# ScalarE makes one of the last chunk's two copies and two of the last six stores

## The chip, the cores and the metric

The kernel runs on one core of a Trainium2 chip. The time is the device time of one execution in microseconds (us), as the median of several runs. The core has five engines that run side by side, each with its own ordered list of instructions: TensorE (PE: matmuls), VectorE (DVE), ScalarE (ACT), GpSimd (POOL) and SyncE (SP). A transfer (DMA) is issued by an engine from its list, here by SP or by ScalarE, and is then carried out by 16 DMA engines that all queues share.

## The reference

Two stages. The first is a linear attention with a sketched feature map; the second takes its output, with the four heads side by side, as 4352 tokens of 128 values and sends them through a two-layer network with the activation h * sigmoid(beta * h):

```
q, k, v: 4 x 4 x 1088 x 32 (batch, heads, sequence, head size);  S1, S2: 8 x 32
phi(x) = outer product of S1 x and S2 x, 64 features
num = phi(q) (phi(k)^T v);  den = phi(q) . sum over the sequence of phi(k);  x = num / (den + 1e-6)
x -> 4352 x 128;  h = x @ w_in (128 x 2048);  g = h / (1 + exp(-beta * h));  out = g @ w_out (2048 x 128)
```

The output is 4352 x 128 in float32.

## The kernel before

Only the end of the second stage matters here. The tokens are worked off in ten chunks (`tok_chk`), numbered 0 to 9: chunks 0, 2 and 9 have 256 tokens, the others 512. Chunk 9 is `LAST`; chunk 8 holds tokens 3584 to 4095, and chunk 9 tokens 4096 to 4351.

For a chunk the 2048 hidden values come as 16 blocks of 128. `W` (line 384) makes the first layer's matmuls for a group of blocks into a PSUM tile `wave` (L393). `S` (line 407) has ScalarE apply Silu to it, giving the fp16 tile `g` (L410). `V` (line 418) adds the second layer's product to the accumulator `moeout`: for chunks 0 to 8 with the weights as the stationary operand (L440), so that the result is feature by token. For chunk 9 the operands are exchanged (L428), the result is token by feature, and its two halves of 128 tokens stand in two PSUM tiles, `moe["acc"][0]` and `moe["acc"][1]`. Within each `V` of chunk 9 the matmuls of the first half come before those of the second.

`y` (`turn_out`, line 453) takes a finished accumulator to an SBUF tile `o_sb`, of which there are two, used in turn. For chunks 0 to 8 it is one 32 x 32 block transpose on VectorE (L463). For chunk 9 it is two plain copies on VectorE, one for each half (L460).

`z` (`store_out`, line 467) sends the oldest tile that has not been sent to the output. Up to chunk 8 it calls `store` (line 362), which issues four DMAs on SP, one for each group of 32 partitions (L369); a chunk that crosses the end of a batch entry is cut in two and takes eight. Chunk 8 does not cross one and takes four of 64 KB. For chunk 9, `z` issues two DMAs on SP, one for each half, 64 KB each (L474).

The order of the work is written out by hand: `SEQ` (line 890) is a list of tokens, each of which calls one of these functions. It fixes the order of each engine's own instructions. Between engines nothing but data holds them: each instruction waits for those whose tiles it reads or overwrites, and these waits are put in from the reads and writes. `y` and `z` work through first-in-first-out lists (`done`, `outs`), so that the k-th `z` stores the chunk that the k-th `y` turned. The list before ends in

```
V W V S W V S S V y z V V y z z
```

where the first `y` is chunk 8's, the first `z` chunk 7's, the second `y` chunk 9's, and the last two `z` are those of chunks 8 and 9. The last `S` stands ahead of all of these.

Of the kernel before, what the change touches and what calls it, by code (L numbers as in the profile page):

```python
# [15 lines left out]
P = 128  # L16
# [3 lines left out]
def kernel(  # L20
# [14 lines left out]
    B, H, S, D = q.shape  # L35
# [24 lines left out]
    tok_chk = []  # L60
# [43 lines left out]
    PE, DVE, ACT, POOL, SP = nc.tensor, nc.vector, nc.scalar, nc.gpsimd, nc.sync  # L104
    DO = {}

    def op(name):
        def put(fn):
            assert name not in DO, name
            DO[name] = fn  # L110
            return fn

        return put
# [244 lines left out]
    LAST = len(tok_chk) - 1  # L358
# [3 lines left out]
    def store(o_sb, t0, nt):  # L362
        c = t0
        while c < t0 + 32 * nt:
            b, r = divmod(c, S)
            n = min(t0 + 32 * nt - c, S - r) // 32
            u = (c - t0) // 32
            for g4 in range(4):
                SP.dma_start(  # L369
                    out=bass.AP(  # L370
                        tensor=out.tensor,
                        offset=out.offset + (b * S + r // 32) * DM + 32 * g4,
                        ap=[[T * DM, 32], [DM, n], [1, 32]],
                    ),
                    in_=o_sb[32 * g4 : 32 * g4 + 32, u : u + n, :],
                )
            c += n * 32
# [74 lines left out]
    @op("y")  # L452
    def turn_out():
        ci, t = done.pop(0)
        t0, tw = tok_chk[ci]
        o_sb = sbA.tile([P, TCH // 32, 32], F32, tag="o_sb", name="o_sb")
        nt = tw // 32
        if ci == LAST:
            for n in range(tw // P):
                DVE.tensor_copy(out=o_sb[:, 4 * n : 4 * n + 4, :].rearrange("p t d -> p (t d)"), in_=t[n][:, :P])  # L460
            outs.append((ci, o_sb, t0, nt))
            return
        DVE.transpose(out=o_sb[:, :nt, :].rearrange("p t d -> p (t d)"), in_=t[:, :tw])  # L463
        outs.append((ci, o_sb, t0, nt))

    @op("z")
    def store_out():
        ci, o_sb, t0, nt = outs.pop(0)
        if ci < LAST:
            store(o_sb, t0, nt)  # L470
            return
        b, r = divmod(t0, S)
        for n in range(nt // 4):
            SP.dma_start(  # L474
                out=bass.AP(
                    tensor=out.tensor,
                    offset=out.offset + (b * S + r // 32 + 4 * n) * DM,
                    ap=[[T * DM, 32], [DM, 4], [1, DM]],
                ),
                in_=o_sb[:, 4 * n : 4 * n + 4, :],  # L480
            )
# [60 lines left out]
    for b in range(B):  # L542
# [57 lines left out]
        if b == 0:  # L600
# [36 lines left out]
            for c, (j0, j1) in (("a", (0, 2)), ("b", (2, NJK))):  # L637
                r = slice(H * j0, H * j1)
                n = H * (j1 - j0)
# [227 lines left out]
    for n, (j0, j1) in enumerate(JRP):  # L867
# [34 lines left out]
        DI3 O33 S V V W y v30 v31 S W S v32 S DS3 W V z W S V W v33 v34 S W V kt3 S W p30 S V t30 W V  # L902
        nd3 S W p33 t33 S S V P31 W V S t31 P32 t32 V W y S n3 V W V V x30 X31 W S S V W V S W S V W S V
        W V W V V S S W W V S S V y W z V W V S S W S V W V W V S W S V W S V W z V S W S V W V S y W S
        V W V S W V S S V y z V V y z z
    """
    for s_ in SEQ.split():
        DO[s_]()
# [29 lines left out]
```

## Time and profile before

| | us |
|---|---|
| median of 3 runs | 109.79 |
| the runs | 109.72, 110.7, 109.79 |
| the profiled execution | 110.03 |
| its span, first to last instruction | 108.2 |
| around the span (110.03 - 108.2) | 1.83 |

In the span, TensorE has matmuls for 98.6 us (91%), ScalarE is busy for 72.8 us (67%), VectorE for 63.4 us (59%) and GpSimd for 33.8 us (31%). TensorE's granted clock is 1.0 throughout.

How to read the lines: times are us from the span's start unless they are marked ns; "L369" is line 369 of the kernel before. "SPq" and "ACTq" are instructions that SP's and ScalarE's sequencers handle themselves, issues of DMAs above all; "ACT" and "DVE" without q are the engines' own work. A timeline line has the start, the length, engine, line, operation, output <- input, and the count of instructions merged; in square brackets stands the idle time before it and what ended it. A line by source or tile has shortest/median/longest ns and the first and last start. "DMA to landing" is the time from the start of a DMA's issue to its completion. In a line of windows the first fields are the stretch and its length, then busy time (and count) of PE, PEld, DVE, ACT and POOL, and at the end the granted clock, the mean busy share of the 16 DMA engines, and GB/s.

### The profile page before, as it was taken

Reading aid. Unit: us, or ns where it says so; the run is one execution under the profiler, and the core shown is the slowest. Engines: PE = TensorE matmul, PEld = TensorE weight load, DVE = VectorE, ACT = ScalarE, POOL = GpSimd, SP = SyncE. Lnnn points to the kernel's source line nnn. Section 1 sums busy time; section 2 is a strip of 40 time slices with the busy share of each in tenths; the row PEclk is TensorE's granted clock in tenths of the full one; section 3 lists DMA queues with packets and bytes.
Section 4 is the critical chain, followed back from the end, with each engine's and each line's share of the span. In section 5 each row is a group of like instructions: output and inputs, shape, how many; then the busy total and the mean of one; then the engine's idle time right before and its main releaser. Section 6 shows DMA issues by size and latency. Waiting matters only on the chain.

```text
span 108.2 us, 2920 instructions
## 1 busy us (share of the span) xinstructions
PE 98.6 (91%) x1205; PEld 55.4 (51%) x1205; DVE 63.4 (59%) x115; ACT 72.8 (67%) x90; POOL 33.8 (31%) x51
## 2 busy tenths in 40 slices
PE   6999969977996999999999999999998999999940
PEld 2443327463653746648545545556554555556830
DVE  3056999999999999999920255807825020110210
ACT  0520001267989755798999746999965999999920
POOL 5002949991893305653910002090000000000000
PEclk9999999999999999999999999999999999999999
DMA  3999999989501451002741224060014005014061
GB/s 76 366 254 373 412 386 247 321 255 357 211 9 27 127 134 23 6 0 48 158 117 32 45 36 64 0 97 21 18 21 69 15 7 84 13 27 70 0 97 49
DMA packets 23517, 12.65 MB, mean 117 GB/s; under 512 B 19408, under 2 KB 21712, under 8 KB 23504
## 3 DMA queue, kind: packets, MB, share of 16 engines
q1 hardware_dynamic: 22896, 11.88, 40.7%
q10 hardware_dynamic: 608, 0.59, 2.2%
q8 instruction: 9, 0.15, 0.6%
q14 instruction: 4, 0.03, 0.1%
HBM read 9.94 MB, written 2.23 MB: 112 GB/s over the span
## 4 chain that ended last, share of the span: by engine, by line
PE 52%; DVE 40%; issue 3%; ACT 1%; DVEq 0%; ACTq 0%
PE wave L393 19%; PE moeout L440 19%; DVE qo L529 7%; PE kvz L267 5%; DVE kp L529 5%; DVE qT L487 4%; DVE kT L487 3%; DVE qt L741 3%; PE nps L756 3%; DVE kab L557 3%; DVE qab L701 3%; PE moeout L428 2%; PE kvs L793 1%; DVE o_sb L463 1%; DVE qm L707 1%
## 5 line engine op out<-in xcount | busy, mean ns | idle before, releaser
L410 ACT ACTIVATE g<-wave 128x1024 f16<-128x1024 f32 x68 | 65.4, 1034 | 10.0 <-PE wave L393 9.9
L393 PE MATMUL wave<-xT,winp 128*128 128x512 f16 (+1 forms) x160 | 40.3, 351 | 1.2 <-DVE winp L332 0.7
L440 PE MATMUL moeout<-g,woutp 128*128 128x512 f16 (+1 forms) x144 | 35.9, 355 | 0.9 <-DVE woutp L346 0.4
L393 PEld LDWEIGHTS <-winp 128*128 128x128 f16 x160 | 21.0, 146 | 14.7 <-issue 2.6
L440 PEld LDWEIGHTS <-woutp 128*128 128x128 f16 x144 | 13.7, 97 | 13.6 <-issue 2.3
L463 DVE STREAM_TRANSPOSE o_sb<-moeout 128x512 f32<-128x512 f32 (+1 forms) x9 | 5.8, 644 | 23.2 <-PE moeout L440 23.2
L529 POOL TENSOR_TENSOR kp<-kab 128x512 f32<-128x512 f32 (+1 forms) x13 | 13.2, 1042 | 12.5 <-DVE kab L557 9.6
L267 PE MATMUL kvz<-idle 128*128 128x384 f16 x41 | 11.0, 412 | 1.1 <-DVE hm L238 1.1
L529 POOL TENSOR_TENSOR qo<-qab 128x512 f32<-128x512 f32 (+1 forms) x7 | 8.8, 1265 | 3.6 <-DVE qab L725 3.5
L529 DVE TENSOR_TENSOR qo<-qab 128x512 f32<-128x512 f32 (+2 forms) x10 | 9.6, 970 | 0.0
L741 DVE STREAM_TRANSPOSE qt<-qo 128x512 f32<-128x512 f32 (+1 forms) x12 | 8.7, 746 | 0.1
L583 ACT COPY gt<-gram 128x32 f32<-128x32 f32 x3 | 0.6, 188 | 11.1 <-PE gram L572 11.1
L529 DVE TENSOR_TENSOR kp<-kab 128x512 f32<-128x512 f32 x7 | 7.6, 1079 | 0.0
L267 PEld LDWEIGHTS <-idle 128*128 128x128 f16 x41 | 4.1, 117 | 6.4 <-issue 4.5
L707 POOL TENSOR_TENSOR qm<-qab 128x288 f32<-128x288 f32 x2 | 1.6, 800 | 17.8 <-DVE qab L701 17.8
L487 DVE STREAM_TRANSPOSE kT<-k 128x1088 f32<-128x1088 f32 x4 | 5.2, 1291 | 3.0 <-DMA k<-in_k_dram 3.0
L346 POOL TENSOR_TENSOR woutp<-w_out_sb,rbeta 128x128 f16<-128x128 f32 x10 | 4.6, 498 | 2.6 <-issue 2.6
L701 DVE STREAM_TRANSPOSE qab<-qps 128x576 f32<-128x576 f32 x6 | 4.3, 758 | 1.5 <-PE qps L687 1.5
L487 DVE STREAM_TRANSPOSE qT<-q 128x1088 f32<-128x1088 f32 x4 | 5.1, 1272 | 0.0
L756 PE MATMUL nps<-qt,nd 32*32 32x288 f32 x192 | 5.0, 412 | 0.0
L557 DVE STREAM_TRANSPOSE kab<-kps 128x288 f32<-128x288 f32 x8 | 3.3, 451 | 2.0 <-PE kps L506 2.0
L793 PEld LDWEIGHTS kvs<-kp,v 128*32 128x32 f32 x216 | 3.3, 109 | 2.4 <-issue 2.4
(82 smaller groups left out, 71.2 us busy)
## 6 DMA issues: line engine op xcount, KB each, us to landing
k<-in_k_dram SPq DMA_DIRECT2D x4, 544.0 KB, 8.2
q<-in_q_dram SPq DMA_DIRECT2D x4, 544.0 KB, 6.9
v<-in_v_dram SPq DMA_DIRECT2D x11, 144.0 KB, 4.5
out_dram<-o_sb SPq DMA_DIRECT2D x18, 64.0 KB, 2.0
beta_bc<-in_moe_beta_dram SPq DMA_DIRECT2D x2, 512.0 KB, 7.8
w_in_sb<-in_moe_w_in_dram SPq DMA_DIRECT2D x2, 512.0 KB, 8.3
w_out_sb<-in_moe_w_out_dram SPq DMA_DIRECT2D x2, 512.0 KB, 8.1
v<-in_v_dram ACTq DMA_DIRECT2D x4, 144.0 KB, 7.0
```

What stands on the lines that cost most here:

```text
L267: PE.matmul(out=kvz[:, P:], lhsT=idle, rhs=cut(idle, [[0, 3], [1, P]]), start=fresh, stop=True, skip_group_check=True,)
L346: eng.tensor_tensor(out=woutp[:, j, :], in0=w_out_sb[:, j, :], in1=cut(rbeta, [[0, P]], j), op=MUL,)
L393: PE.matmul(out=wv[:, jj // per, o : o + tw], lhsT=unit(j0 + jj), rhs=xT[:, t0 : t0 + tw], start=True, stop=True,)
L410: ACT.activation(out=g, in_=wv, func=ACTF.Silu)
L440: PE.matmul(out=moe["acc"][:, :tw], lhsT=woutp[:, j, :], rhs=g[jj], start=(j == 0), stop=(j == NJ - 1),)
L463: DVE.transpose(out=o_sb[:, :nt, :].rearrange("p t d -> p (t d)"), in_=t[:, :tw])
L487: DVE.transpose(out=dst[:, t0:t1].rearrange("p t s -> p (t s)"), in_=src[:, t0:t1].rearrange("p t d -> p (t d)"),)
L529: eng.tensor_tensor(out=cut(dst[b][:, j0:j1], [[F, n], [R, R], [1, R]]), in0=cut(t, [[step, n], [1, R], [0, R]], j0 * H * step), in1=cut(t ...
L557: DVE.transpose(out=cut(KAB[b], [[H * R, NJK], [NJK * H * R, 2], [1, 2 * R]], 2 * R * pi), in_=PS["kps", b][:, pi, :JW],)
L701: DVE.transpose(out=cut(QAB[b], [[4 * R, 2], [4 * R * H, NJK], [1, 4 * R]], 2 * 4 * R * n), in_=PS["qps", b][n][:, :, :JW],)
L741: DVE.transpose(out=QT[b][:, j0:j1].rearrange("p j h c s -> p (j h c s)"), in_=QO[b][:, j0:j1].rearrange("p j h f -> p (j h f)"),)
L756: PE.matmul(out=tiles[g // 2][32 * h : 32 * h + 32, g % 2, : 32 * nj], lhsT=nd_of(b, h, fc, g), rhs=QT[b][rows, :nj, h, fc, :], start=(fc ...
```

## The change

- Of the four DMAs with which chunk 8 is stored, the fourth (partitions 96 to 127) is issued by ScalarE instead of SP.
- Of the two copies of chunk 9, the second is made by ScalarE instead of VectorE.
- Of the two DMAs of chunk 9, the second is issued by ScalarE instead of SP.
- In `SEQ`, chunk 8's `z` moves ahead of the last two `V` and chunk 9's `y`. On SP, VectorE and TensorE the order stays as it was. On ScalarE the fourth DMA of chunk 8 thereby stands ahead of the copy of chunk 9.

```diff
             for g4 in range(4):
-                SP.dma_start(
+                eng = ACT if g4 == 3 and t0 == tok_chk[LAST - 1][0] else SP
+                eng.dma_start(
                     out=bass.AP(
...
             for n in range(tw // P):
-                DVE.tensor_copy(out=o_sb[:, 4 * n : 4 * n + 4, :].rearrange("p t d -> p (t d)"), in_=t[n][:, :P])
+                eng = (DVE.tensor_copy, ACT.copy)[n % 2]
+                eng(out=o_sb[:, 4 * n : 4 * n + 4, :].rearrange("p t d -> p (t d)"), in_=t[n][:, :P])
...
         for n in range(nt // 4):
-            SP.dma_start(
+            (SP, ACT)[n % 2].dma_start(
                 out=bass.AP(
...
-        V W V S W V S S V y z V V y z z
+        V W V S W V S S V y z z V V y z
```

## The prediction

> **What bounds the kernel now.** I read the page first (span, engines), then the chain that ended last, then the timeline of the last 7 us, then the stores' own rows, what SP waits for at the end, and the DMA share in short windows. The chain of work, in order of time, ends like this (start us, us, what):
>
> ```profile
> 102.17 1.65 PE moeout L428 x28
> 103.82 0.02 issue
> 103.84 0.52 DVE o_sb L460 x2
> ```
>
> So TensorE sets the time up to 103.82, VectorE's two copies follow, and the chain of compute stops at 104.36. The span is 108.2: another 3.8 us go to things that are not compute. The timeline of the tail names them (start us, us, engine, line, count):
>
> ```profile
> 101.72 0.72 DVE L463 STREAM_TRANSPOSE o_sb<-moeout 128x512 f32<-128x512 f32 x1 [6.62 <-PE moeout L440]
> 102.00 2.02 PE L428 MATMUL moeout<-woutp,g 128*128 128x128 f16 x32
> 102.27 1.08 ACT L410 ACTIVATE g<-wave 128x1024 f16<-128x1024 f32 x1
> 102.46 0.32 SPq L369 DMA_DIRECT2D out_dram<-o_sb  x1
> 103.90 0.51 SPq L369 DMA_DIRECT2D out_dram<-o_sb  x1
> 104.06 0.29 DVE L460 COPY o_sb<-moeout 128x128 f32<-128x128 f32 x1
> 104.51 1.33 SPq L474 DMA_DIRECT2D out_dram<-o_sb  x2
> ```
>
> The four stores of chunk 8 (L369) keep SP issuing from 102.46 to 104.41. The first copy of chunk 9 was finished before that: 103.84 plus the 0.29 that one copy takes is 104.13. Yet its store is issued only at 104.51, when SP is free, and the second one behind it. The rows of the stores by line, chunk 8's (L369) and chunk 9's (L474), in ns, each with the time from issue to landing, and what SP waits for at the very end (in total, times, longest):
>
> ```profile
> L369 SPq DMA_DIRECT2D out_dram<-o_sb x4: 315/496/507, 102.5 to 103.9; - x4
> DMA to landing us min/median/max: 1.8/1.9/2.0
> ...
> L474 SPq DMA_DIRECT2D out_dram<-o_sb x2: 577/614/652, 104.5 to 105.3; - x2
> ...
> DMA to landing us min/median/max: 1.9/2.0/2.0
> ```
>
> ```profile
> SPq L933 <- DMA out_dram<-o_sb: 1.3, 2, 0.7
> ```
>
> The second store starts at 104.51 + 1.33 - 0.577 = 105.26 and lands 1.9 later, at 107.16. SP waits for exactly that, and what is left, 108.2 - 107.16 = 1.04 us, is the closing exchange between the engines. The end of this kernel is therefore: last copy, then SP's queue of issues, then one store's latency, then 1.04 us. The DMA engines do not set it (all of the core's DMA, window, length, granted clock, share, GB/s):
>
> ```profile
> 105.60:105.80 0.20, 0.00 (x0) 0.00 (x0) 0.00 (x0) 0.00 (x0) 0.00 (x0) 1.00 0.00 0
> 105.80:106.00 0.20, 0.00 (x0) 0.00 (x0) 0.00 (x0) 0.00 (x0) 0.00 (x0) 1.00 0.78 233
> 106.00:106.20 0.20, 0.00 (x0) 0.00 (x0) 0.00 (x0) 0.00 (x0) 0.00 (x0) 1.00 0.35 95
> 106.20:106.40 0.20, 0.00 (x0) 0.00 (x0) 0.00 (x0) 0.00 (x0) 0.00 (x0) 1.00 0.00 0
> 106.60:106.80 0.20, 0.00 (x0) 0.00 (x0) 0.00 (x0) 0.00 (x0) 0.00 (x0) 1.00 0.76 215
> ```
>
> They idle before each of chunk 9's two stores; these come when they are issued, not when there is room.
>
> **The change, part by part.** Three things move to ScalarE: one copy, one issue of chunk 8, one issue of chunk 9. The rows with which I price them (groups by line and form; then timeline rows):
>
> ```profile
> L834 ACT COPY nd<-kvz 128x64 f32<-128x64 f32 x1 | 0.2, 212 | 1.1 <-PE kvz L822 1.1
> L862 ACT COPY qf<-qfps 128x256 f32<-128x256 f32 x1 | 0.4, 378 | 0.0
> L246 ACT ACT_TABLE_LOAD x1 | 1.3, 1283 | 3.1 <-issue 3.1
> ```
>
> ```profile
> 18.30 0.25 PE L592 MATMUL wps<-gt,s2b 128*32 128x8 f32 x8
> 18.61 0.17 ACT L678 COPY qw<-wps 128x8 f32<-128x8 f32 x1 [0.60 <-PE wps L592]
> ```
>
> *The fourth store of chunk 8.* It leaves SP and goes to ScalarE's queue, ahead of the copy there. It waits for the transpose, 101.72 + 0.72 = 102.44. Queued behind it on ScalarE are only the new copy and the new store; the last Silu (102.27) is ahead of it. So it can be issued at about 102.46, beside SP's first one, and is over long before the copy is needed at 104.02. It removes the 0.51 us at 103.90 from SP: SP is free at 103.86 instead of 104.41. On the landing side it costs nothing: it comes earlier than it did.
>
> *The second copy.* Its matmuls end at 102.00 + 2.02 = 104.02; on VectorE it started at 104.06. ScalarE starts a copy 0.06 after its matmuls (18.30 + 0.25 = 18.55 to 18.61), so 104.08. Between the copies of 64 and of 256 columns (212 and 378 ns) a copy of 128 comes to 212 + 64 x 0.865 = 267 ns: it ends at 104.35, as VectorE's did (104.06 + 0.29 = 104.35). No gain and no loss in itself: the copies were not what the end waited for. The one table load of the whole program, with copies and Silu mixed before, says that a copy after a Silu loads no table; if it did, 1.28 us would fall on the path.
>
> *The two stores of chunk 9.* The first stays on SP and starts when its copy is done, 104.13 + 0.02 (the step from the transpose's end at 102.44 to the issue at 102.46) = 104.15; it lands 2.0 later, at 106.15. The second is issued by ScalarE at 104.35 + 0.02 = 104.37 instead of 105.26: **0.89 us earlier**. That is the whole of the change's worth; it is now the last thing to land.
>
> *What it runs beside.* No row of before shows two stores issued at once from two queues. The nearest rows are loads. Once ScalarE's queue and SP's overlap like this:
>
> ```profile
> 20.24 0.45 ACTq L163 DMA_DIRECT2D v<-in_v_dram  x1
> ...
> 20.42 0.33 SPq L148 DMA_DIRECT2D q<-in_q_dram  x1
> ```
>
> SP's issue lies 0.27 us inside ScalarE's and takes 0.33, hardly more than the shortest store's issue on an empty queue (315 ns, L369). At the start of the program two loads on each queue overlap, and one such pair on SP alone stands below them; after that come two windows of the DMA share at that time (1.13 and 1.02, before GB/s: the DMA engines were full):
>
> ```profile
> L163 SPq DMA_DIRECT2D v<-in_v_dram x2: 432/688/945, 1.7 to 2.1; - x2
> L163 ACTq DMA_DIRECT2D v<-in_v_dram x2: 373/669/965, 1.7 to 2.1; - x2
> ...
> L163 SPq DMA_DIRECT2D v<-in_v_dram x2: 430/430/430, 9.7 to 10.1; - x2
> ```
>
> ```profile
> 1.70:2.10 0.40, 0.40 (x3) 0.23 (x2) 0.24 (x4) 0.00 (x0) 0.40 (x5) 1.00 1.13 177
> ...
> 2.60:3.10 0.50, 0.50 (x3) 0.29 (x2) 0.00 (x0) 0.01 (x1) 0.00 (x0) 1.00 1.02 287
> ```
>
> The first of each took what it takes alone (432 and 373), the second of each about 0.52 more (945 and 965 against 430). So the price of the overlap lies between 0 and 0.52 us. The two stores of chunk 9 also share the DMA engines: one of them keeps all 16 busy for 0.2 x (0.78 + 0.35) = 0.23 us, so sharing costs 0 to 0.23. I take 0.10 for both together: chunk 9's two stores are the first on each queue after a pause, like the pair that was not stretched.
>
> Sum, against the profiled execution of 110.03 (span 108.2 and 1.83 around it): 110.03 - 0.89 + 0.10 = 109.24. That execution was 0.24 over the median of the runs shown (109.79), so the forecast is 109.79 - 0.79 = **109.0 us**, 0.7% faster. The forecast's own range goes from no overlap price and a landing 0.1 quicker (an issue that is not queued behind another: 1.8 instead of 1.9), 109.79 - 0.99 = 108.8, to the price of 0.3, 109.2.
>
> **The rivals.** (a) *The issues take turns.* If only one queue's issue can be worked on at a time, it does not matter on which engine they stand: chunk 8's four end at about 104.41 as now, chunk 9's two follow in turn, the second starts at 105.26 or, with SP's gap of 0.10 between them (105.26 - 104.51 - 0.652) gone, at 105.16. Gain 0 to 0.1: 109.7 to 109.8. For it speaks the stretched second pair (945, 965), against it the first pair and the issue at 20.42. [...]
>
> (b) *Partly.* Each issue that overlaps another is stretched as the second pair was, by 0.52; only the last one counts on the path. Gain 0.89 - 0.52 = 0.37: 109.4. The same rows speak for it; against it, that the DMA engines were full then (1.13, 1.02), so that the stretch may have been the data's.
>
> (c) *Slower: ScalarE's queue lands late.* The page has for the same load, by queue:
>
> ```profile
> v<-in_v_dram SPq DMA_DIRECT2D x11, 144.0 KB, 4.5
> v<-in_v_dram ACTq DMA_DIRECT2D x4, 144.0 KB, 7.0
> ```
>
> and for the loads that both queues issued between 1.6 and 3.0, SP's first and ScalarE's second:
>
> ```profile
> DMA to landing us min/median/max: 7.2/7.5/7.8
> ...
> DMA to landing us min/median/max: 6.6/6.8/7.0
> ```
>
> If a store on ScalarE's queue lands 7.0/4.5 = 1.56 times as late, the last one takes 1.9 x 1.56 = 3.0 and lands at 104.37 + 3.0 = 107.37, 0.2 later than now: 110.0. It decides from a landing time of 107.16 - 104.37 = 2.8 us on. Against it: where both queues loaded at the same time, ScalarE's landed sooner (6.6 to 7.0 against 7.2 to 7.8).
>
> (d) *It does not do what it says.* If the waits were set for the tile o_sb as a whole, ScalarE's copy would wait for VectorE's (104.13), and SP's store for both copies. Price 104.15 - 104.08 = 0.07: 109.1, inside the forecast. Against it, two engines write one tile at once here:
>
> ```profile
> 18.12 1.07 POOL L529 TENSOR_TENSOR qo<-qab 128x512 f32<-128x512 f32 x1
> ...
> 18.49 0.99 DVE L529 TENSOR_TENSOR qo<-qab 128x256 f32<-128x256 f32 x1
> ```
>
> **How the numbers follow.** The forecast with (d) gets 0.60, (b) 0.17, (a) 0.15, (c) 0.05, a gain above 1.0 that I have no mechanism for 0.03. 109.0 is the likeliest case's. The range goes from 108.75 to 109.85: it takes in (b) and (a) and leaves out (c) and the ends, about 0.1. One per cent, 1.1 us, is about what a measurement of this kernel can tell from no change. The forecast (0.7%), (b) and (a) are all within it, and (c) at its price too. Over 1% faster needs less than 108.69, which takes 0.2 us more than the 0.89 that can be saved at the issue: 0.10, since landing times vary by that much. Over 1% slower needs ScalarE's landing at 3.9: 0.03. Within 1%: 0.87.
>
> **What would show it.** Right: an issue of L369 on ScalarE's queue at about 102.5, three on SP that end near 103.9; VectorE's one copy at 103.84 and ScalarE's at 104.1; the store on SP at 104.15 to 104.2, that on ScalarE's queue at 104.35 to 104.45; the last landing near 106.4; a span near 107.4; all before 101.7 as it was. Wrong: issues on the two queues that lengthen each other to 0.9 us or more (a, b), a landing over 2.8 us on ScalarE's queue (c), ScalarE's copy starting only after VectorE's has ended (d), or a gain above 1.1, which would mean that something besides the issue moved.

## The result, and the profile after

The changed kernel takes 109.18 us as the median of 20 runs, against 109.8 us for the kernel before in 20 runs (medians 0.62 apart). The ratio is 0.9943 with a 95% interval of 0.9923 to 0.9963: 0.6% faster, within the 1% that was set as the bound, but clear of no change. The forecast was 109.0 us. A few of the runs lie 1.5% or more above the fastest, several at a lower granted clock, and are left out of this and every other ratio; the profiled execution of 113.23 in the table of the experiments (granted clock 0.932) is one of them. The profiled executions are 110.03 and 109.12; of these 0.91 us, 0.22 lie ahead of the last matmul, where nothing was changed, and 0.69 behind it.

The timeline of the tail after, as in the prediction's second fence (L370 are chunk 8's stores, L476 chunk 9's, L462 its copies):

```profile
101.50 0.72 DVE L465 STREAM_TRANSPOSE o_sb<-moeout 128x512 f32<-128x512 f32 x1 [6.62 <-PE moeout L441]
101.78 2.02 PE L429 MATMUL moeout<-woutp,g 128*128 128x128 f16 x32
102.25 1.41 SPq L370 DMA_DIRECT2D out_dram<-o_sb  x3
102.25 0.38 ACTq L370 DMA_DIRECT2D out_dram<-o_sb  x1
103.62 0.29 DVE L462 COPY o_sb<-moeout 128x128 f32<-128x128 f32 x1 [1.40 <-PE moeout L429]
103.84 0.27 ACT L462 COPY o_sb<-moeout 128x128 f32<-128x128 f32 x1 [0.71 <-PE moeout L429]
103.94 0.65 SPq L476 DMA_DIRECT2D out_dram<-o_sb  x1
104.14 0.65 ACTq L476 DMA_DIRECT2D out_dram<-o_sb  x1
```

All times are to be read from the last matmul's end, now 101.78 + 2.02 = 103.80, before 104.02. Every step stands where the prediction put it. SP and ScalarE issue chunk 8's stores at the same moment; the copies end as before; the last store is issued 104.14 - 103.80 = 0.34 after the last matmul instead of 105.26 - 104.02 = 1.24. That is 0.90 sooner. And the two issues of chunk 9 lie beside each other for 0.45 us.

The same stores by line, with the landing times that the trace has (those issued by SP):

```profile
L370 SPq DMA_DIRECT2D out_dram<-o_sb x3: 317/488/512, 102.2 to 103.1; - x3
L370 ACTq DMA_DIRECT2D out_dram<-o_sb x1: 378/378/378, 102.2 to 102.2; - x1
...
DMA to landing us min/median/max: 2.3/2.5/2.7
```

```profile
L476 SPq EVENT_SEMAPHORE  x1: 17/17/17, 103.7 to 103.7; - x1
L476 SPq DMA_DIRECT2D out_dram<-o_sb x1: 648/648/648, 103.9 to 103.9; - x1
L476 ACTq DMA_DIRECT2D out_dram<-o_sb x1: 654/654/654, 104.1 to 104.1; - x1
...
DMA to landing us min/median/max: 2.0/2.0/2.0
```

Two things to see. The issues are not stretched by each other: 317, 488 and 512 ns on SP against 315, 496 in the middle and 507 before, and 648 beside 654 ns where SP alone took 652. But the landings are: chunk 8's stores take 2.3 to 2.7 us instead of 1.8 to 2.0. The DMA engines are fuller meanwhile (last two columns: busy share, GB/s):

```profile
103.00:103.50 0.50, 0.50 (x12) 0.43 (x9) 0.00 (x0) 0.13 (x1) 0.00 (x0) 1.00 0.53 71
103.50:104.00 0.50, 0.31 (x6) 0.13 (x3) 0.29 (x1) 0.16 (x1) 0.00 (x0) 1.00 1.02 143
104.00:104.50 0.50, 0.00 (x0) 0.00 (x0) 0.00 (x0) 0.11 (x1) 0.00 (x0) 1.00 0.98 139
104.50:105.00 0.50, 0.00 (x0) 0.00 (x0) 0.00 (x0) 0.00 (x0) 0.00 (x0) 1.00 0.99 144
105.00:105.50 0.50, 0.00 (x0) 0.00 (x0) 0.00 (x0) 0.00 (x0) 0.00 (x0) 1.00 0.60 148
105.50:106.00 0.50, 0.00 (x0) 0.00 (x0) 0.00 (x0) 0.00 (x0) 0.00 (x0) 1.00 0.50 142
```

Before, half a microsecond in the middle of the same data looked like this:

```profile
103.50:104.00 0.50, 0.50 (x9) 0.35 (x7) 0.16 (x1) 0.00 (x0) 0.00 (x0) 1.00 0.76 119
```

The four issues of chunk 8 are over within 1.41 us on two queues, instead of 1.95 on one, and while their data flows the engines' share is 1.02, 0.98 and 0.99 instead of 0.76. That a store's data then waits longer for those ahead of it is my reading; no row shows it by itself.

The last store is ScalarE's, and its landing is read from SP, which waits for it at the very end (L935; before L933). SP checks five completions one after the other. Here are these checks after, and then those from 107 us on before:

```profile
L935 SPq EVENT_SEMAPHORE  x5: 28/28/617, 105.6 to 106.5; - x5
L935 SPq DRAIN  x2: 7/7/7, 106.6 to 106.6; - x2
```

```profile
L933 SPq EVENT_SEMAPHORE  x4: 28/28/28, 107.2 to 107.4; - x4
L933 SPq DRAIN  x2: 7/7/7, 107.5 to 107.5; - x2
```

In windows of 0.01 us the long check (617 ns) starts at 105.64 and ends at 106.26: the store of 104.14 has landed after **2.12 us**. Before, SP's wait lies in no check's own time; the first of the four checks starts at 107.20, 1.94 after the issue at 105.26 (the trace has that landing itself, at 1.9). So the sum is 0.90 - (2.12 - 1.94) = 0.72 us; the closing (checks and exchange between the engines) is 1.04 us after and 1.00 before, as one more check stands behind the last landing, which leaves 0.68 of the 0.69.

### The profile page after: what moved, and what is told of

Its sections match the earlier page's. It is cut to its first block, busy times and chain, and to the rows that moved or that the text cites. A ratio compares the mean times of both kernels' runs of the same rounds, so it can differ in the third digit from the quotient of the medians.

```text
span 107.3 us, 2924 instructions
## 1 busy us (share of the span) xinstructions
PE 98.9 (92%) x1205; PEld 55.6 (52%) x1205; DVE 62.8 (59%) x114; ACT 73.1 (68%) x91; POOL 33.8 (32%) x51
## 4 chain that ended last, share of the span: by engine, by line
PE 45%; DVE 37%; DMA 8%; issue 3%; SPq 2%; ACT 1%; DVEq 0%; ACTq 0%
PE wave L394 19%; PE moeout L441 19%; DMA k<-in_k_dram 8%; DVE qo L531 7%; DVE kp L531 5%; DVE kT L489 3%; DVE qt L743 3%; PE nps L758 3%; DVE qab L703 3%; DVE qT L489 3%; DVE kab L559 2%; PE moeout L429 2%; PE kvs L795 1%; DVE o_sb L465 1%; SPq L163 1%
## 5 line engine op out<-in xcount | busy, mean ns | idle before, releaser
L531 DVE TENSOR_TENSOR kp<-kab 128x512 f32<-128x512 f32 x7 | 7.1, 1013 | 0.0
```

The source lines that it names most:

```text
L531: eng.tensor_tensor(out=cut(dst[b][:, j0:j1], [[F, n], [R, R], [1, R]]), in0=cut(t, [[step, n], [1, R], [0, R]], j0 * H * step), in1=cut(t ...
```

## The experiments

The time of a whole execution scatters ahead of the last matmul: in the table its end goes from 102.98 to 104.93 (without the 107.60), though the edits are all behind it, but for an order of columns in the last two kernels. So each kernel is read by what the change touches: the time of its profiled execution less the end of its last matmul, called the rest. It was 110.03 - 104.02 = 6.01 before and 109.12 - 103.80 = 5.32 after. The expectations also speak of the tail, from the same point to the end of the span; the rest has in addition the 1.8 us around the span. Of the execution of 113.23, which has 3.6 us more ahead of its last matmul, only the rest is used; its granted clock from 105.6 to 107.6 was 1.0.

| kernel | execution | last matmul ends | rest | against before | timed ratio, interval |
|---|---|---|---|---|---|
| before | 110.03 | 104.02 | 6.01 | | |
| changed | 109.12 | 103.80 | 5.32 | -0.69 | 0.9943, 0.9923 to 0.9963 |
| changed, again | 109.22 | 103.91 | 5.31 | -0.70 | not timed |
| second store of chunk 9 only | 109.5 | 104.07 | 5.43 | -0.58 | 0.9992, 0.9954 to 1.0029 |
| fourth store of chunk 8 only | 113.23 | 107.60 | 5.63 | -0.38 | 0.9975, 0.9942 to 1.0008 |
| copy only | 109.78 | 103.81 | 5.97 | -0.04 | 0.9991, 0.9955 to 1.0028 |
| both stores, no copy | 109.07 | 103.77 | 5.30 | -0.71 | 0.9913, 0.9881 to 0.9944 |
| all, old order | 108.28 | 102.98 | 5.30 | -0.71 | 0.9938, 0.9899 to 0.9976 |
| without chunk 8's stores | 108.29 | 103.15 | 5.14 | -0.87 | 0.9932, 0.9898 to 0.9967 |
| without chunk 9's first store | 108.8 | 103.56 | 5.24 | -0.77 | 0.9915, 0.9888 to 0.9943 |
| last store alone | 109.87 | 104.93 | 4.94 | -1.07 | not timed |
| stores in halves | 109.41 | 103.55 | 5.86 | -0.15 | 1.0016, 0.9978 to 1.0055 |
| one store | 108.5 | 103.22 | 5.28 | -0.73 | 0.9941, 0.9908 to 0.9975 |
| one store, early fourth | 108.36 | 102.99 | 5.37 | -0.64 | 0.9944, 0.9917 to 0.9971 |

The theory under test: the end is set by when the last store can be issued; the issues of two queues do not hold each other up; what was lost of the gain was lost in landing. The rivals: the issues take turns, the parts need each other, or the copy on ScalarE does it.

**The changed kernel once more.**

> The changed kernel once more, to see how far the time after the last matmul's end repeats: 5.32 within 0.05 if differences of 0.1 between these kernels mean something, further off if they do not.

5.31 against 5.32. On this one repeat I read differences of 0.1 as real and none under 0.05.

**One part at a time.** The next four are edits of the kernel before, all others of the changed kernel. The second store alone:

```diff
-            SP.dma_start(
+            (SP, ACT)[n % 2].dma_start(
```

> Of the change only one line: the second store of chunk 9 is issued by ScalarE. The copies stay on VectorE and chunk 8's four stores on SP. Tail here means the time from the end of the last matmul to the end of the span; it was 4.2 us before (108.2 - 104.02) and 3.5 in the changed kernel (107.3 - 103.80). Issue theory (what counts is when the last store can be issued, landing about 2.0 to 2.1, closing 1.04): the second store goes at 0.36 after the last matmul, the first when SP is free at 0.49 and lands 2.0 later, so the end is 0.49 + 2.0 + 1.04: tail 3.5 to 3.6, nearly the whole gain. Rival, all parts are needed (SP's own queue must be relieved first): tail 3.8 to 3.9. Rival, issues take turns: 4.1 to 4.2.

```profile
102.51 1.96 SPq L369 DMA_DIRECT2D out_dram<-o_sb  x4
103.89 0.52 DVE L460 COPY o_sb<-moeout 128x128 f32<-128x128 f32 x2 [1.40 <-PE moeout L428]
104.43 0.63 ACTq L474 DMA_DIRECT2D out_dram<-o_sb  x1
104.56 0.65 SPq L474 DMA_DIRECT2D out_dram<-o_sb  x1
```

The tail is 107.7 - 104.07 = 3.6, as the issue theory has it: the rest is 0.58 shorter, most of the 0.69. ScalarE's store goes at 0.36 after the last matmul; the last to go is now SP's, at 104.56, 0.49 after it, because SP still issues four stores of chunk 8. The timed ratio of 0.9992 does not show this gain: 0.58 of 110 would be 0.9947, just outside its interval. I hold to the rest, which shows each step, and leave it open why the timed runs fell short.

The fourth store of chunk 8 alone:

```diff
-                SP.dma_start(
+                eng = ACT if g4 == 3 and t0 == tok_chk[LAST - 1][0] else SP
+                eng.dma_start(
```

> Only the fourth store of chunk 8 moves to ScalarE; both copies stay on VectorE and both stores of chunk 9 on SP. Issue theory: SP is free 0.55 sooner, its first store goes when the copy is done (0.13 after the last matmul), the second 0.75 behind it at 0.88, landing 1.9 to 2.0: tail 0.88 + 1.95 + 1.04 = 3.85 to 3.9, about half of the gain. Rival, the fourth store is the part that matters: 3.5. Rival, issues take turns: 4.2.

```profile
106.04 1.40 SPq L370 DMA_DIRECT2D out_dram<-o_sb  x3
106.04 0.38 ACTq L370 DMA_DIRECT2D out_dram<-o_sb  x1
107.42 0.52 DVE L461 COPY o_sb<-moeout 128x128 f32<-128x128 f32 x2 [1.41 <-PE moeout L429]
107.74 1.33 SPq L475 DMA_DIRECT2D out_dram<-o_sb  x2
```

Tail 111.5 - 107.60 = 3.9, as expected: SP's first store goes at 107.74 - 107.60 = 0.14 after the last matmul, the second still waits its turn behind it. Half of the gain, 0.38.

The copy alone:

```diff
-                DVE.tensor_copy(out=o_sb[:, 4 * n : 4 * n + 4, :].rearrange("p t d -> p (t d)"), in_=t[n][:, :P])
+                eng = (DVE.tensor_copy, ACT.copy)[n % 2]
+                eng(out=o_sb[:, 4 * n : 4 * n + 4, :].rearrange("p t d -> p (t d)"), in_=t[n][:, :P])
```

> Only the second copy of chunk 9 moves to ScalarE; all stores stay on SP. Issue theory: both copies are done before SP is free, so tail 4.2 as before, time within 0.2 per cent of before. Rival, two engines copying at once bring the end forward: tail 3.9 to 4.1.

5.97 against 6.01: nothing. The other side of it, both stores moved and the copy left on VectorE (the two store diffs above together):

> Both store moves without the copy: chunk 8's fourth store and chunk 9's second store on ScalarE's queue, both copies on VectorE, the order list as before. Issue theory: VectorE's second copy ends at the same time as ScalarE's would, so tail 3.5 as in the changed kernel. Rival, the copy on ScalarE matters because its own store waits for no other engine: tail 3.6 to 3.7.

```profile
103.58 0.52 DVE L461 COPY o_sb<-moeout 128x128 f32<-128x128 f32 x2 [1.41 <-PE moeout L429]
103.90 0.65 SPq L475 DMA_DIRECT2D out_dram<-o_sb  x1
104.13 0.63 ACTq L475 DMA_DIRECT2D out_dram<-o_sb  x1
```

5.30, as the changed kernel. The last issue comes 104.13 - 103.77 = 0.36 after the last matmul with VectorE's copy, 0.34 with ScalarE's. The copy's move is worth nothing. The two store moves are worth 0.58 and 0.38 alone and 0.7 together: each frees the same last issue, so their gains do not add up.

**The order.** All three moves, with the list's last line as before (`y z V V y z z`):

> All three moves, but the order list as before, so that on ScalarE the copy of chunk 9 stands ahead of chunk 8's fourth store. Theory: a store waits behind a copy that has not started, so the fourth store goes only when the copy starts (0.04 after the last matmul instead of 1.55 before it), takes 0.38, and the last store follows at about 0.45 instead of 0.34: tail 3.6 to 3.7 against 3.5. Rival, ScalarE's issues pass a waiting copy: fourth store at its old early place, tail 3.5.

```profile
103.02 0.27 ACT L462 COPY o_sb<-moeout 128x128 f32<-128x128 f32 x1 [0.71 <-DMA out_dram<-o_sb]
103.03 0.34 ACTq L370 DMA_DIRECT2D out_dram<-o_sb  x1
103.12 0.65 SPq L476 DMA_DIRECT2D out_dram<-o_sb  x1
103.41 0.64 ACTq L476 DMA_DIRECT2D out_dram<-o_sb  x1
```

The step is as expected: the fourth store stands behind a copy that waits, and goes when that copy starts (103.03, the last matmul ended at 102.98). The bracket names a DMA as what released the copy, but the copy starts 0.04 after the matmuls, as in the changed kernel, where it names TensorE. The last store goes at 0.43 instead of 0.34. But the cost that I expected, a tail of 3.6 to 3.7, did not come: 106.5 - 102.98 = 3.5, rest 5.30. What was lost at the issue came back in the landing. SP's checks at the end of this kernel:

```profile
L935 SPq EVENT_SEMAPHORE  x5: 27/28/28, 105.4 to 105.7; - x5
```

In windows of 0.01 us the first starts at 105.42: the last store lands 2.01 after its issue instead of 2.12, and 2.44 after the last matmul, against 106.26 - 103.80 = 2.46 in the changed kernel. The two stores of chunk 9 are issued 103.41 - 103.12 = 0.29 apart here and 0.20 apart there. So in the changed kernel the last store is no longer held by its own issue alone: 0.09 of the 0.90 won there is lost again in the landing, behind chunk 9's first store. (The landings of chunk 8's stores that the trace has are 1.8 to 1.9 in this kernel, not 2.3 to 2.7.)

**Where the 0.18 of landing went.** Three kernels leave out stores. Without chunk 8's:

```diff
         if ci < LAST:
-            store(o_sb, t0, nt)
+            if ci < LAST - 1:
+                store(o_sb, t0, nt)
             return
```

> The changed kernel without the four stores of chunk 8 (512 tokens of the output are not written). In the changed kernel the last store took 2.1 from issue to the end of SP's wait, 0.2 more than the last one before. Theory, the price comes from chunk 9's two stores sharing the engines: still 2.1, tail 3.5. Rival, chunk 8's data, still flowing until 105.15, is what they queue behind: 1.9 or less, tail 3.3 or less.

Without chunk 9's first (`for n in range(1, nt // 4)` in `store_out`):

> The changed kernel without the first store of chunk 9 (128 tokens of the output are not written); chunk 8's four are there. Theory, the two stores of chunk 9 delay each other: landing of the last 1.9, tail 3.3. Rival, chunk 8's data delays it, or ScalarE's queue lands later by itself: still 2.1, tail 3.5.

With both left out:

> The changed kernel without chunk 8's stores and without chunk 9's first (640 tokens of the output are not written), so that the last store has the engines to itself. Measured as time of the execution after the last matmul's end (changed kernel 5.32, without chunk 8's stores 5.14, without chunk 9's first 5.24). If the overlap is the whole of the price: 5.06 to 5.12, the landing 1.9 as for the last store before the change. If ScalarE's queue lands later by itself: 5.2 or more.

SP's checks at the end, in the first (with the closing exchange's first) and in the third kernel:

```profile
L936 SPq EVENT_SEMAPHORE  x4: 17/28/1452, 104.1 to 106.0; - x4
L936 SPq DRAIN  x2: 7/7/7, 105.7 to 105.8; - x2
```

```profile
L936 SPq DRAIN  x2: 7/7/7, 107.3 to 107.4; - x2
L936 SPq EVENT_SEMAPHORE  x1: 28/28/28, 107.3 to 107.3; - x1
```

Read in windows of 0.01 us, the last store takes from its issue until SP's check sees it (the end of a check that waited, or the start of one that took no more than its 28 ns), and SP then takes to its first drain:

| kernel | issue | landed | landing | from there to the drain |
|---|---|---|---|---|
| before | 105.26 | 107.20 | 1.94 | 107.46: 0.26 |
| changed | 104.14 | 106.26 | 2.12 | 106.56: 0.30 |
| changed, again | 104.25 | 106.38 | 2.13 | 106.67: 0.29 |
| all, old order | 103.41 | 105.42 | 2.01 | 105.74: 0.32 |
| without chunk 8's stores | 103.49 | 105.58 | 2.09 | 105.74: 0.16 |
| without chunk 9's first | 103.90 | 105.93 | 2.03 | 106.23: 0.30 |
| last store alone | 105.26 | 107.27 | 2.01 | 107.34: 0.07 |

My expectations took the whole tail for landing, and that was wrong. Without chunk 8's stores the tail is 106.5 - 103.15 = 3.35 and the rest 0.18 shorter, which by the expectation would make chunk 8's data the cause; the last store alone is at 4.94, below both of the values expected. But the landing is nearly the same (2.09 against 2.12). Shorter is the closing: behind the check that waits there are two more instead of four, and they start 0.06 to 0.07 us apart. The landing falls by 0.09 without chunk 9's first store, and by 0.11 with the engines quite free. Of the 0.18 by which the last landing is longer than before, about 0.1 is the company of chunk 9's first store, 0.20 ahead; with that store 0.29 ahead, in the old order, it is gone. The other 0.07 is there without any company, 2.01 against 1.94, and an issue that is longer by about as much goes with it: 0.64 here, 0.577 for the second in a row before. SP's own two stores of chunk 9 before differ in the same way: the one issued in 0.652 landed in 2.0, the one issued in 0.577 in 1.9.

**Two tries for a better end.** Halves: each store of chunk 9 as two of 64 partitions, one on each queue.

```diff
-            (SP, ACT)[n % 2].dma_start(
+            for i in range(2):
+                (SP, ACT)[i].dma_start(
...
-                in_=o_sb[:, 4 * n : 4 * n + 4, :],
+                    in_=o_sb[64 * i : 64 * i + 64, 4 * n : 4 * n + 4, :],
```

> The changed kernel with each store of chunk 9 cut in two halves of 64 partitions, one on SP and one on ScalarE at the same time. If an issue of half the partitions takes half the time (0.33 instead of 0.65), the last data is handed over at about 0.34 + 0.33 after the last matmul instead of 0.34 + 0.65, tail 3.2 to 3.4, better than the changed kernel. If an issue takes the same 0.65 whatever its size, the second pair starts at about 0.80 (0.14 + 0.65) and tail is 3.9 to 4.0. On the issue theory the second is as likely: chunk 8's stores of 32 partitions show 0.32 alone and 0.50 in a row.

```profile
L477 SPq DMA_DIRECT2D out_dram<-o_sb x2: 570/591/612, 103.7 to 104.4; - x2
L477 ACTq DMA_DIRECT2D out_dram<-o_sb x2: 634/744/854, 103.7 to 104.4; - x2
```

The second outcome, tail 107.6 - 103.55 = 4.05, a little over it. Half the partitions take nearly as long to issue (612 and 570 on SP, in this order; 652 and 577 for the whole in the kernel before), the second pair starts at 104.4, and 5.86 gives back nearly all. Here the two queues' issues may also have delayed each other, ScalarE's up to 854; no other run of chunk 9's stores shows that.

One store: the halves of chunk 9 hold even and odd tokens, so that a partition has 1 KB in one piece, and ScalarE issues all of it once. In the first of two kernels chunk 8's four stores are back on SP; in the second the fourth is on ScalarE.

```diff
-                    in_=cut(PS["num", b][i], [[P, n // P], [32, 4], [1, 32]], 512 + 32 * nj - n),
+                    in_=cut(PS["num", b][i], [[32, n // P], [64, 4], [1, 32]], 512 + 32 * nj - n),
...
+        ACT.dma_start(
...
+                ap=[[T * DM, 32], [2 * DM, 4], [1, 2 * DM]],
+            ),
+            in_=o_sb[:, :nt, :],
+        )
```

> Chunk 9 leaves in one store of 128 KB, issued by ScalarE after both copies; chunk 8's four stay on SP. For that the two halves of chunk 9 hold the even and the odd tokens, so that a partition sends 1 KB in one piece (the column order of the last chunk in xT changes with it). Measured as time of the execution after the last matmul's end: before 6.01 (110.03 - 104.02), changed kernel 5.32 (109.12 - 103.80), without chunk 8's stores 5.14, without chunk 9's first store 5.24. If what counts is only when the last issue can be made and how much lies in the engines' way: issue at 0.35 as in the changed kernel, chunk 8's four in turn as before, half the packets in chunk 9: 5.15 to 5.30, at or ahead of the changed kernel. If one store of 128 KB lands later than two of 64 KB from two queues: 5.4 to 5.6.

The first line has a store of chunk 7 and chunk 8's four in one:

```profile
97.63 5.98 SPq L370 DMA_DIRECT2D out_dram<-o_sb  x5
...
103.27 0.27 ACT L462 COPY o_sb<-moeout 128x128 f32<-128x128 f32 x1 [0.71 <-DMA out_dram<-o_sb]
103.56 0.63 ACTq L475 DMA_DIRECT2D out_dram<-o_sb  x1
```

> The same one store for chunk 9 on ScalarE, with chunk 8's fourth store on ScalarE too, early. If chunk 8's early fourth store only crowds the engines (its neighbours landed in 2.3 to 2.7 instead of 1.8 to 2.0) and SP is no longer in the way: the same as with chunk 8's four on SP, within 0.1. If chunk 8's data ending sooner helps: 0.1 to 0.2 better.

5.28 with chunk 8's four on SP and 5.37 with the fourth on ScalarE, on both sides of the changed kernel's 5.32, and timed ratios of 0.9941 and 0.9944: no version beats it clearly. In the first, three checks stand behind the last landing, 0.06 to 0.07 us apart; if the second has a fourth, as the changed kernel has, that is 0.07 of the 0.09 between the two, an estimate. Twice the bytes are issued in the same 0.63 us. Once SP is out of the way of the last store, moving chunk 8's fourth brings nothing.

## Why the prediction was right, and one term that was off

- *The last store is issued 0.89 sooner.* Measured 0.90, though the old order shows that the last 0.09 of it brought nothing. The step rests on SP's four issues being what the finished copy waited for; the two parts done alone (issue at 0.36 and at 0.14 after the last matmul) show both halves of it.
- *The fourth store of chunk 8 goes at the transpose's end, beside SP's first.* Both at 102.25, 0.03 after the transpose. *On the landing side it costs nothing* was wrong for its neighbours: they land 2.3 to 2.7 us after their issue instead of 1.8 to 2.0, while the engines' share is 1.0 instead of 0.76. It was not on the path.
- *The copy brings nothing by itself.* So it did (5.97 against 6.01; 5.30 without it against 5.32). It took the 0.27 us that were forecast and started 0.04 after the matmuls, where 0.06 was forecast.
- *The overlap costs 0.10.* This is the term that was mis-sized. It is 0.18 in landing: 0.1 behind chunk 9's first store, within the 0 to 0.23 given for sharing the engines (whether it arises there or in handing over the data, no run here shows), and 0.07 that goes with an issue of 0.65 where I had carried over 1.9 from one that took 0.577. That first-on-the-queue issue was in the row I quoted (577/614/652); I took the landing of the wrong one. With 0.18 in place of 0.10 the sum is 109.08.
- *The remaining 0.1 between that and 109.18* is 0.04 of longer closing (1.04 against 1.00), which the prediction held constant; the rest of it I cannot place: by the time after the last matmul the gain is 0.69, by the medians 0.62, and the interval of the ratio (0.41 to 0.85 us) holds both.
- *The rivals.* Issues that take turns (a), or stretch by 0.52 (b), did not show in the changed kernel: SP's issues kept their lengths, and ScalarE's last, 0.45 us of it beside SP's, took 654 ns where it takes 638 alone (without chunk 8's stores and chunk 9's first), and it started 0.03 after its copy; taking turns would have put it off or made it longer by about those 0.45. The one issue as long as (b) feared is ScalarE's 854 in the kernel with halves. ScalarE's queue does not land late (c): 2.01 alone, far from 2.8. The waits were set by halves, not by the tile (d): ScalarE's copy started at 103.84, before VectorE's ended at 103.91.

## What to carry to other kernels

At the end of a kernel look at the queue that issues the last stores, not only at the data: here the last result lay finished while SP still issued the stores ahead of it, 0.5 to 0.65 us each. Give the last store to an engine that has nothing left to issue, or make it one store; of three moves here that one was worth 0.58 of 0.69 us, by the time after the last matmul. Sooner than about 0.3 us behind the store ahead of it brought nothing more here. Measure such a change from the last instruction that it doesn't touch, since the whole execution scatters by more than it is worth.

## What the hardware showed besides

- The issue of a store took nearly as long for 32 KB from 64 partitions (0.57 and 0.61 on SP) as for 64 KB (0.58 and 0.65 on SP) and 128 KB (0.63 on ScalarE) from 128.
- SP's checks of further completions behind the last landing start 0.06 to 0.07 us apart: from landing to the first drain it took 0.07, 0.16 and 0.30 us with no, two and four such checks.
- Issuing chunk 8's stores from two queues raised the DMA engines' share from 0.76 to 1.0 but ended its data hardly sooner (at about 105.2, 1.4 us after the last matmul, against 105.5, 1.5 us after it): chunk 9's data then follows at once (share 0.60 and 0.50 behind it), where before there was a gap (share 0.00 from 105.6 to 105.8).
